# Strassen's seven products in the first product of the second FFN, on one Trainium2 core

## The chip, the cores and the metric

The kernel runs on one core of one Trainium2 chip. The metric is the device time of one execution in microseconds (us); the time before is the median of three runs. Engines are named as in the profile: PE is the matrix engine (TensorE), PEld its weight loads, DVE the vector engine (VectorE), ACT the scalar engine (ScalarE), SP the engine that issues the DMAs (SyncE).

## The reference

Three stages over 4608 tokens (8 batches of 576), a model width of 512 and an FFN width of 2048, all in fp32:

```
# linear attention, per batch and head, then RMS norm
kv  = einsum('bhsd,bhse->bhde', k, v);  out = einsum('bhsd,bhde->bhse', q, kv)
x   = out / sqrt(mean(out*out, -1) + 1e-6) * g_norm
# first FFN
h = x @ w_in;  g = P(h) / Q(|h|);  x = g @ w_out
# second FFN (the change is here)
h = x @ w_in                        # 4608x512 @ 512x2048
g = where(h >= 1, h, where(h <= -1, 0, (h + 1)**2 / 4))
return g @ w_out                    # 4608x2048 @ 2048x512
```

## The kernel before

**Tiles.** The tokens are cut into 9 blocks of T = 512 (`NB`), the FFN width into 16 slices of 128 (`NF`, index `f`), the model width into 4 slices of 128 (`KT`). An fp32 operand is kept as two fp32r tiles, a rounded high part and the rest (`xh`/`xl`, `wih`/`wil`, `woh`/`wol`, `gh`/`gl`), and a product of two operands takes three matmuls: high by high, high by low, low by high.

**The second FFN.** `ffn_step(1, j, f, s)` (L540) does for a block j and a slice f: 4 x 3 matmuls into one bank `h` (L548 to L550), the nonlinearity (a clamp on DVE, L577; a square on ACT; a maximum on DVE, L581), the split of g into `gh` (ACT) and `gl` (DVE, L199), and then 4 x 3 matmuls into the four banks `acc0` to `acc3` (L606 to L608), which sum over f. This second product lags by `LAG` = 3 steps: in(f) is followed by out(f-3). After f = 15 the banks are copied by ACT and stored. Everything in PSUM is 8 banks: two `h`, one `o`, one `m`, four `acc`; `o` and `m` serve the attention and are idle in the second FFN.

**Weights.** They come as 64-bit floats. `weight(ph, f, half, key)` (L254) loads one 512 KB slice into a `raw` tile, turns it into fp32 with integer and ACT instructions in a tile `t`, and splits it. For the second FFN (`ph` = 1) that takes one ACT conversion (L271), on DVE a shift (L274), the sign (L277) and the low bits (L282), the high part on ACT (L311) and the low part on DVE (L320). A slice's buffers become free as the last block of the first FFN passes it, so that the second FFN's weights are decoded during that block and during block 0 of the second FFN. All weights then stay in SBUF.

**Order.** No order of instructions is written by hand. Each operation is given to `Program` with its engine, a cost, a key (its due time in steps of 24 matmuls) and the buffers that it reads and writes. Buffers of one name form a ring of so many buffers, and within a ring they are handed on in the order of the buffers' keys: a later one waits for every operation on the one that it replaces. A list scheduler then plays the program through with its costs and, on each engine, always takes the ready operation of the smallest key:

```python
    LATENCY = 0.15
    ...
            while pending[e] and pending[e][0][0] <= s:
                i = heappop(pending[e])[1]
                heappush(ready[e], (self.ops[i][2], i))
            i = heappop(ready[e])[1]
```

The order that results is fixed for each engine, and each engine works through its own in order. All DMAs are issued by SP, in its order too. `NS1` = 144 is the key of the second FFN's first step. Inputs of the second FFN come back from DRAM (`x2d`) through three `io` buffers and are split by `x2_split` (L529); a split is one ACT instruction (high part) and one on DVE (low part).

Of the kernel before, what the change touches and what calls it, by code (L numbers as in the profile page):

```python
# [131 lines left out]
def kernel(  # L132
# [28 lines left out]
    T = 512  # L161
# [7 lines left out]
    const = ctx.enter_context(tc.tile_pool(name="const", bufs=1))  # L169
    sb = ctx.enter_context(tc.tile_pool(name="sb", bufs=1))  # L170
    psum = ctx.enter_context(tc.tile_pool(name="psum", bufs=1, space=bass.MemoryType.PSUM))

    RINGS = {
        "wih": NF, "wil": NF, "woh": NF, "wol": NF + 1, "raw": 4, "dec": 2, "io": 3, "xh": KT, "xl": KT,
        "gh": 2, "gl": 2, "ah": 1, "u": 2, "t": 2, "r": 2, "a1": 1, "a2": 1, "a3": 1, "a4": 1,
    }
    PS_RINGS = {"h": 2, "o": 1, "m": 1, "acc0": 1, "acc1": 1, "acc2": 1, "acc3": 1}
    count = [0]
# [75 lines left out]
    def weight(ph, f, half, key):  # L254
# [18 lines left out]
        def shift():  # L273
            nc.vector.tensor_scalar(out=t(), in0=t(), scalar1=3, scalar2=None, op0=ALU.logical_shift_left)  # L274

        def sign():
            nc.vector.scalar_tensor_tensor(  # L277
                out=t(), in0=word(1), scalar=-0x80000000, in1=t(), op0=ALU.bitwise_and, op1=ALU.bitwise_or
            )

        def low():
            nc.vector.scalar_tensor_tensor(  # L282
                out=t(), in0=word(0), scalar=29, in1=t(), op0=ALU.logical_shift_right, op1=ALU.bitwise_or
            )

        def low_bits():
# [11 lines left out]

        load(key, raw, (w1, w2)[ph][f, half], 1.4)
        op(ACT, 0.57, key, bias, [raw], [t])  # L300
        if ph == 0:

            lb = new("gl", key, I32)
            op(ACT, 0.57, key, low_bits, [raw], [lb])
            op(DVE, C_TT, key, shift_low, [lb], [t])
            op(DVE, C_TT, key, sign, [raw], [t])
        else:
            op(DVE, C_TS, key, shift, [], [t])
            op(DVE, C_TT, key, sign, [raw], [t])
            op(DVE, C_TT, key, low, [raw], [t])  # L310
        op(ACT, C_SB, key, lambda: nc.scalar.activation(out=hi(), in_=t().bitcast(F32), func=AF.Copy), [t], [hi])  # L311
        if keep:
            w32[f] = t
            wsb[ph, f, half] = (hi, None)
        else:
            weight_low(ph, f, half, key, t, hi)

    def weight_low(ph, f, half, key, t, hi):
        lo = new(("wil", "wol")[half], key, F32R)
# [2 lines left out]
        ), [t, hi], [lo])  # L322
        wsb[ph, f, half] = (hi, lo)


    xs = {}
    kvs = {}
# [85 lines left out]
    def x_split(e, xh, xl, key):  # L413
        activate(key, xh, e)
        subtract(key, xl, e, xh)
# [203 lines left out]

    NS1 = NB * NF

    order = [(0, 0), (1, 0), (2, 0)]
    for f in range(3, NF):
# [89 lines left out]
```

## Time and profile before

| | |
|---|---|
| median of three runs | 1680.24 us (1680.13 to 1683.94) |
| span of the profiled execution | 1677.8 us, first to last instruction |
| its own time | not printed; the median is 2.4 us above the span |
| busy: PE, DVE, ACT | 1655.2, 1187.1, 969.4 us |
| moved by DMA | 94.29 MB, 56 GB/s over the span |

Busy time is the time in which an engine has an instruction in hand; on PE and DVE consecutive instructions overlap, so that the distance between two starts is shorter than what one instruction lasts. A releaser is what ended an idle time: `<-DVE u L577` is an instruction of DVE on line 577 that wrote u.

### The profile page before, as it was taken

What the parts mean: (1) busy time and instruction counts of PE and PEld (TensorE: products, weight loads), DVE (VectorE), ACT (ScalarE), POOL (GpSimd) and SP (SyncE); (2) the same over time, 40 slices, a digit from 0 to 9 for tenths busy, and PEclk for the clock granted to TensorE, in tenths of its full rate; (3) what the DMA queues carried; (4) which work ended last, traced back from release to release, by engine and by line L of the source; (5) the groups of instructions that cost most, each with busy time, mean ns of one, the idle gap of its engine ahead of it and who ended that gap; (6) DMA issues with size and microseconds to landing.
All of it is one profiled execution on the core that took longest, in us unless ns stands there. A gap on an engine that the chain in (4) does not pass through costs nothing.

```text
span 1677.8 us, 20972 instructions
## 1 busy us (share of the span) xinstructions
PE 1655.2 (99%) x7888; PEld 1334.3 (80%) x7888; DVE 1187.1 (71%) x1864; ACT 969.4 (58%) x1633; POOL 0.2 (0%) x4
## 2 busy tenths in 40 slices
PE   6999999999999999999999999999999999999999
PEld 3666788888888888888888888888888888888887
DVE  5999999999999999999999953434343434343333
ACT  7987888887878788888886532323232323232222
POOL 0000000000000000000000000000000000000000
PEclk9999999999999999999999999999999999999999
DMA  8966101010101001010215410101010101000000
GB/s 276 308 215 190 39 19 39 19 38 19 38 20 38 11 11 49 26 45 13 76 51 169 144 51 0 51 1 51 0 51 1 50 1 51 1 25 7 1 26 25
DMA packets 51685, 94.29 MB, mean 56 GB/s; under 512 B 12992, under 2 KB 21056, under 8 KB 51584
## 3 DMA queue, kind: packets, MB, share of 16 engines
q1 hardware_dynamic: 51584, 92.96, 16.9%
q8 instruction: 62, 1.02, 0.2%
q14 instruction: 39, 0.32, 0.1%
HBM read 73.14 MB, written 19.79 MB: 55 GB/s over the span
## 4 chain that ended last, share of the span: by engine, by line
PE 95%; ACT 2%; DMA 2%; SPq 0%; DVE 0%; issue 0%; ACTq 0%
PE h L548 15%; PE h L549 15%; PE h L550 15%; PE acc L608 8%; PE acc L606 8%; PE acc L607 8%; PE acc L602 7%; PE acc L603 7%; PE acc L604 7%; PE acc L600 2%; DMA raw<-in_w_dram 1%; PE m L356 1%; PE o L501 1%; ACT a L194 0%; DMA wol<-in_kv_dram 0%; DMA ab_sb<-in_a_dram 0%
## 5 line engine op out<-in xcount | busy, mean ns | idle before, releaser
L548 PE MATMUL h<-xh,wih 128*128 128x512 f32 x1152 | 455.9, 396 | 3.7 <-DVE a L208 2.0
L549 PE MATMUL h<-xl,wih 128*128 128x512 f32 x1152 | 448.5, 389 | 0.0
L550 PE MATMUL h<-xh,wil 128*128 128x512 f32 x1152 | 448.4, 389 | 0.0
L194 ACT ACTIVATE u<-u 128x512 f32<-128x512 f32 x144 | 90.9, 631 | 352.2 <-DVE u L577 352.1
L548 PEld LDWEIGHTS h<-xh,wih 128*128 128x128 f32 x1152 | 216.1, 188 | 55.7 <-issue 4.2
L549 PEld LDWEIGHTS h<-xl,wih 128*128 128x128 f32 x1152 | 216.4, 188 | 47.2 <-issue 3.2
L550 PEld LDWEIGHTS h<-xh,wil 128*128 128x128 f32 x1152 | 216.2, 188 | 45.2
L577 DVE TENSOR_SCALAR u<-h 128x512 f32<-128x512 f32 x144 | 99.4, 691 | 180.3 <-PE h L550 180.3
L606 PE MATMUL acc<-woh,gh 128*128 128x512 f32 x576 | 224.1, 389 | 0.0
L607 PE MATMUL acc<-wol,gh 128*128 128x512 f32 x576 | 224.1, 389 | 0.0
L608 PE MATMUL acc<-woh,gl 128*128 128x512 f32 x576 | 224.1, 389 | 0.0
L602 PE MATMUL acc<-gh,woh 128*128 128x512 f32 x512 | 200.0, 391 | 0.0
L603 PE MATMUL acc<-gh,wol 128*128 128x512 f32 x512 | 199.3, 389 | 0.0
L604 PE MATMUL acc<-gl,woh 128*128 128x512 f32 x512 | 199.2, 389 | 0.0
L208 DVE SCALAR_TENSOR_TENSOR u<-u,r 128x512 f32<-128x512 f32 x272 | 186.9, 687 | 12.1 <-ACT r L194 8.3
L199 DVE TENSOR_TENSOR gl<-t,gh 128x512 fp32r<-128x512 f32 x144 | 99.6, 692 | 133.7 <-ACT gh L194 133.7
L194 ACT ACTIVATE gh<-t 128x512 fp32r<-128x512 f32 x144 | 90.9, 631 | 135.2 <-PE acc L607 134.3
L581 DVE TENSOR_TENSOR t<-u,h 128x512 f32<-128x512 f32 x144 | 99.0, 688 | 97.1 <-ACT u L194 97.1
L608 PEld LDWEIGHTS acc<-woh,gl 128*128 128x128 f32 x576 | 108.1, 188 | 22.6
L606 PEld LDWEIGHTS acc<-woh,gh 128*128 128x128 f32 x576 | 108.2, 188 | 22.4
L607 PEld LDWEIGHTS acc<-wol,gh 128*128 128x128 f32 x576 | 108.0, 188 | 22.4
L194 ACT ACTIVATE ah<-h 128x512 f32<-128x512 f32 x144 | 85.8, 596 | 66.2 <-PE h L550 65.1
(105 smaller groups left out, 2125.0 us busy)
## 6 DMA issues: line engine op xcount, KB each, us to landing
raw<-in_w_dram SPq DMA_DIRECT2D x64, 512.0 KB, 3.8
x2d<-io SPq DMA_DIRECT2D x36, 256.0 KB, 2.4
io<-x2d SPq DMA_DIRECT2D x36, 256.0 KB, 3.0
raw<-in_qT_dram SPq DMA_DIRECT2D x56, 128.0 KB, 3.0
raw<-in_kv_dram SPq DMA_DIRECT2D x12, 512.0 KB, 5.3
out_dram<-r SPq DMA_DIRECT2D x18, 256.0 KB, 2.0
out_dram<-a SPq DMA_DIRECT2D x18, 256.0 KB, 2.2
woh<-in_kv_dram SPq DMA_DIRECT2D x12, 256.0 KB, 5.2
```

What stands on the lines that cost most here:

```text
L194: op(ACT, cost, key, lambda: nc.scalar.activation(out=out(), in_=in_(), func=func, **{k: v() if callable(v) else v for k, v in kw.items()} ...
L199: op(DVE, C_TT, key, lambda: nc.vector.tensor_tensor(out=out(), in0=x(), in1=hi().bitcast(F32), op=ALU.subtract), [x, hi], [out])
L208: op(DVE, C_STT if callable(add) else C_TT, key, lambda: nc.vector.scalar_tensor_tensor(out=out(), in0=x(), scalar=add() if callable(add) ...
L548: nc.tensor.matmul(out=h(), lhsT=whi()[:, c], rhs=xh(), start=(p == 0), stop=False)
L549: nc.tensor.matmul(out=h(), lhsT=whi()[:, c], rhs=xl(), start=False, stop=False)
L550: nc.tensor.matmul(out=h(), lhsT=wlo()[:, c], rhs=xh(), start=False, stop=(p == KT - 1))
L602: nc.tensor.matmul(out=o(), lhsT=wohi()[:, c], rhs=gh(), start=first, stop=False)
L603: nc.tensor.matmul(out=o(), lhsT=wolo()[:, c], rhs=gh(), start=False, stop=False)
L604: nc.tensor.matmul(out=o(), lhsT=wohi()[:, c], rhs=gl(), start=False, stop=last)
L606: nc.tensor.matmul(out=o(), lhsT=gh()[:, c], rhs=wohi(), start=first, stop=False)
L607: nc.tensor.matmul(out=o(), lhsT=gh()[:, c], rhs=wolo(), start=False, stop=False)
L608: nc.tensor.matmul(out=o(), lhsT=gl()[:, c], rhs=wohi(), start=False, stop=last)
```

## The change

Blocks 1 to 8 of the second FFN are taken in four groups of two (block 0 stays as it was), and the slices in eight pairs. For a pair of slices, the two halves of the model width and the two blocks, the first product is a 2 x 2 by 2 x 2 product of blocks, done with seven products (Strassen's scheme in Winograd's form) of 2 x 3 matmuls each, into the banks `h`, `o` and `m`, which DVE reads and adds between the products (`ffn2_pair`). Four of the seven left operands are sums and differences of weight blocks. They are made once (`combine`), from the fp32 weights that are kept in DRAM (`td`), and are stored with the plain ones in DRAM (`wd`); each group streams all 56 tiles of 256 KB back through the `wih` ring (`stream`). The right operands are sums and differences of token blocks (`x_combinations`). Both blocks' g fall out of one pair, but there are only four `acc` banks. So one block's g goes on to the second product at once and the other's is kept in `raw` tiles and taken at the end of the half (`ffn2_group`): in the first eight slices the first block's is used and the second's kept, in the other eight the reverse, and the first block's two halves are added at the end. In `weight`, the second FFN's decode now takes the first FFN's path: the shift and one of the two bit operations on DVE give way to a second ACT conversion (L289) and one DVE instruction (L295). `kvbd` moves into the rings `kv0` and `kv1`, which are used again later.

```diff
+    wd = dram.tile([NPAIR, 7, P, T], F32, name="wd")
+    td = dram.tile([NF, P, T], F32, name="td")
...
-    kvbd = [fixed(f"kvbd{i}", [P, NP, P]) for i in range(2)]
+    kvbd = [new(f"kv{i}", -100, shape=(P, NP, P)) for i in range(2)]
...
-        t = new("wol" if keep else "dec", key, I32)
+        t = new("wol" if keep else f"a{1 + f % 4}" if ph and not half else "dec", key, I32)
...
+        lb = new(f"kv{half}", 0.5 * (key - NS1) - 20 + NS1, I32) if ph else new("gl", key, I32)
+        op(ACT, 0.57, key, low_bits, [raw], [lb])
+        op(DVE, C_TT, key, shift_low, [lb], [t])
+        op(DVE, C_TT, key, sign, [raw], [t])
...
+        if ph and not half:
+            store_plain(f, key + 0.3)
+            tds[f] = prog.buf(None)
+            op(SP, 0.7, key + 0.3, lambda: nc.sync.dma_start(out=td[f], in_=t().bitcast(F32)), [t], [tds[f]])
...
+    def combine(i, key):
+        a, b = (new(f"a{1 + (2 * i + n) % 4}", key) for n in range(2))
+        for t, f in ((a, 2 * i), (b, 2 * i + 1)):
+            load(key - 1, t, td[f], reads=[tds[f]])
+        s12, s34 = new("r", key), new("r", key + 0.01)
...
+        add(s12, 0, b, 0, b, 1, ALU.add, [b])
+        add(s12, 1, s12, 0, a, 0, ALU.subtract, [s12, a])
+        add(s34, 0, a, 0, b, 0, ALU.subtract, [a, b])
+        add(s34, 1, a, 1, s12, 1, ALU.subtract, [a, s12])
+        for n in range(4):
+            s, c = (s12, s34)[n // 2], q[n % 2]
+            stage = new("ah" if i < 2 else "dec", key + 2 + 0.01 * n, F32R)
... # high half on ACT (256 wide), low half on DVE (256 wide)
+            store(key, i, (S1 + n, S1 + n + 1), ...)
...
+    STREAM = (A11, S2, S1, A12, S3, A22, S4)
+    def stream(g, i, key):
+        for n, c in enumerate(STREAM):
+            t = new("wih", key + 7 + 0.01 * n, F32R)
+            op(SP, 0.7, key + 0.01 * n, lambda t=t, c=c: nc.sync.dma_start(out=t().bitcast(F32), in_=wd[i, c]),
+               [wds[i, c]], [t])
+            ws[g, i, c] = t
+    def x_combinations(g, key):
... # B11, T2, T1 in the wil ring, B21, T3, T4, B22 in xh and xl
+            split(B11, b11)
+            t1, t2 = (new("dec", k + 6 + 0.1 * n) for n in range(2))
+            sub(t1, b12, b11)
+            b22 = fetch(jb, 2 + i, 2)
+            sub(t2, b22, t1)
+            split(T2, t2)
+            split(T1, t1)
+            b21 = fetch(ja, 2 + i, 3)
+            split(B21, b21)
+            sub(b12, b22, b12)
+            split(T3, b12)
+            t4 = new(f"kv{i}", k + 4)
+            sub(t4, b21, t2)
...
+    def ffn2_pair(g, i, key):
+        banks = [new(r, key) for r in ("h", "o", "m")]
+        a, b, c = banks
+        v1, u2, u3 = new("t", key), new("kv0", key), new("kv1", key)
... # product(): 2 x 3 matmuls, cost 1.36, key + 0.01 * n;  add(): DVE, out = x + bank
+        product(0, a, A11, B11, True)
+        product(1, b, S2, T2, True)
+        product(2, c, S1, T1, True)
+        activate(key, v1, a, cost=C_PS)
+        add(u2, v1, b)
+        product(3, a, A12, B21, False)
+        product(4, b, S3, T3, False)
+        add(u3, v1, b)
+        add(u3, u3, c)
+        product(5, b, A22, T4, False)
+        product(6, c, S4, B22, False)
+        add(v1, v1, b)
+        add(u2, u2, c)
+        return (a, u2), (v1, u3)
...
+    def ffn2_group(g, s0):
+        ja, jb = 1 + 2 * g, 2 + 2 * g
+        STEP, LUMP = 2.92, 11.7
...
+        for half in range(2):
+            s = s0 + half * NF
+            for q in range(NPAIR // 2):
+                i = half * (NPAIR // 2) + q
+                k = s + STEP * q - 1.0
+                whole = new("raw", k + 3, shape=(P, 2 * T))
+                rows = ffn2_pair(g, i, k)
+                for n in range(2):
+                    f = 2 * i + n
+                    now, later = rows[n] if half == 0 else rows[n][::-1]
+                    ko = k + 3.3 + 1.4 * n
+                    keep = Half(whole, slice(n * T, (n + 1) * T))
+                    e = nonlinear(now, None, k + 0.5)
...
+                    ffn2_out(e, f, o4[0 if half == 0 else 1], ko, ...)
+                    kept.append((f, nonlinear(later, keep, k + 0.6)))
+            k = s + LUMP + 1.5
... # the four banks are copied by ACT, then the kept slices' second product
+            for n, (f, e) in enumerate(kept):
+                ffn2_out(e, f, o, k + 0.53 * n, n == 0, half == 1 and f == NF - 1)
...
-    for j in range(NB):
-        s0 = NS1 + j * NF
-        for p in range(KT):
-            x2_split(j, p, s0 - NF + 3 + 3 * p)
-        for f in range(NF):
-            ffn_step(1, j, f, s0 + f)
+    for p in range(KT):
+        x2_split(0, p, NS1 - NF + 3 + 3 * p)
+    for f in range(NF):
+        ffn_step(1, 0, f, NS1 + f)
+    for g in range((NB - 1) // 2):
+        s0 = NS1 + NF + 2 * NF * g
+        x_combinations(g, s0 - 6)
+        if g == 0:
+            for i in range(NPAIR):
+                combine(i, s0 + 2.0 * i - 5)
+        for i in range(NPAIR):
+            stream(g, i, s0 + (i // 4) * NF + 2.92 * (i % 4) - 7)
+        ffn2_group(g, s0)
```

`store_plain` stores A11, A12 and A22 (the plain blocks, high and low parts side by side) from the decoded tiles. `ffn2_out` is the split of g and the 4 x 3 matmuls of the second product as before, `nonlinear` the clamp, square and maximum as before.

## Rows read from the trace of the kernel before

**Rows 1.** The page's totals (busy us, share) and granted clock by slice.
```profile
PE 1655.2 (99%) x7888; PEld 1334.3 (80%) x7888; DVE 1187.1 (71%) x1864; ACT 969.4 (58%) x1633; POOL 0.2 (0%) x4
...
PEclk9999999999999999999999999999999999999999
```
**Rows 2.** The chain that ended last, by engine.
```profile
PE 95%; ACT 2%; DMA 2%; SPq 0%; DVE 0%; issue 0%; ACTq 0%
```
**Rows 3.** Busy time by stretch: PE, PEld, DVE, ACT, POOL; clock, DMA share, GB/s.
```profile
790.00:882.00 92.00, 92.00 (x408) 76.17 (x407) 91.47 (x152) 76.63 (x128) 0.00 (x0) 1.00 0.17 58
882.00:968.00 86.00, 86.00 (x382) 71.19 (x380) 83.86 (x150) 52.24 (x87) 0.00 (x0) 1.00 0.46 153
...
1011.00:1674.00 663.00, 663.00 (x2926) 548.64 (x2924) 265.30 (x388) 182.06 (x298) 0.00 (x0) 1.00 0.06 20
```
**Rows 4.** PE in order of time: start us, us, engine, line, operands.
```profile
963.92 0.39 PE L548 MATMUL h<-xh,wih 128*128 128x512 f32 x1
...
966.64 0.39 PE L606 MATMUL acc<-woh,gh 128*128 128x512 f32 x1
...
1301.20 0.39 PE L548 MATMUL h<-xh,wih 128*128 128x512 f32 x1
...
1303.92 0.39 PE L606 MATMUL acc<-woh,gh 128*128 128x512 f32 x1
...
1673.61 0.39 PE L608 MATMUL acc<-woh,gl 128*128 128x512 f32 x1
```
**Rows 5.** One step across engines, in order of time.
```profile
1303.69 0.39 PE L550 MATMUL h<-xh,wil 128*128 128x512 f32 x1
...
1304.12 0.69 DVE L577 TENSOR_SCALAR u<-h 128x512 f32<-128x512 f32 x1 [1.53 <-PE h L550]
...
1304.90 0.63 ACT L194 ACTIVATE u<-u 128x512 f32<-128x512 f32 x1 [3.04 <-DVE u L577]
...
1305.57 0.69 DVE L581 TENSOR_TENSOR t<-u,h 128x512 f32<-128x512 f32 x1 [0.76 <-ACT u L194]
```
**Rows 6.** DVE in order of time, around block 0's end.
```profile
940.03 0.42 DVE L274 TENSOR_SCALAR dec<-dec 128x512 int32<-128x512 int32 x1
940.37 0.69 DVE L199 TENSOR_TENSOR gl<-t,gh 128x512 fp32r<-128x512 f32 x1
940.97 0.68 DVE L320 TENSOR_TENSOR wil<-dec,wih 128x512 fp32r<-128x512 f32 x1
...
960.53 0.69 DVE L320 TENSOR_TENSOR wil<-dec,wih 128x512 fp32r<-128x512 f32 x1
...
973.36 0.68 DVE L199 TENSOR_TENSOR xl<-io,xh 128x512 fp32r<-128x512 f32 x1
973.96 0.68 DVE L577 TENSOR_SCALAR u<-h 128x512 f32<-128x512 f32 x1
975.40 0.69 DVE L581 TENSOR_TENSOR t<-u,h 128x512 f32<-128x512 f32 x1 [0.76 <-ACT u L194]
```
**Rows 7.** Groups of DVE instructions, 882 to 968: busy us, mean ns.
```profile
L274 DVE TENSOR_SCALAR dec<-dec 128x512 int32<-128x512 int32 x23 | 9.7, 421 | 0.0
```
**Rows 8.** DMA issues: KB each, median us to landing.
```profile
raw<-in_w_dram SPq DMA_DIRECT2D x64, 512.0 KB, 3.8
x2d<-io SPq DMA_DIRECT2D x36, 256.0 KB, 2.4
io<-x2d SPq DMA_DIRECT2D x36, 256.0 KB, 3.0
...
woh<-in_kv_dram SPq DMA_DIRECT2D x12, 256.0 KB, 5.2
```
**Rows 9.** Busy time by stretch, at the kernel's start.
```profile
10.00:20.00 10.00, 6.61 (x67) 4.41 (x67) 1.38 (x2) 2.67 (x6) 0.00 (x0) 1.00 0.94 313
...
60.00:80.00 20.00, 20.00 (x136) 12.58 (x134) 20.00 (x34) 19.90 (x38) 0.00 (x0) 1.00 0.99 332
```
**Rows 10.** Groups of ACT instructions, whole span: busy us, mean ns.
```profile
L289 ACT ACTIVATE gl<-raw 128x512 int32<-128x512 uint16 x32 | 21.4, 670 | 0.0
```
**Rows 11.** Busy time of 900 to 920, and SP's issues there.
```profile
900.00:920.00 20.00, 20.00 (x90) 16.57 (x89) 18.07 (x33) 11.87 (x21) 0.00 (x0) 1.00 0.69 230
...
902.04 0.32 SPq L616 DMA_DIRECT2D x2d<-io  x1
902.46 0.86 SPq L248 DMA_DIRECT2D io<-x2d  x2
```

More of the change, by code (lines that the diff above doesn't have):

```diff
@@ L618, in ffn_step, with fetch, sub, split @@
                     x2s[j, m] = stored
-    NS1 = NB * NF
+    ws = {}
+    xc = {}
+    B11, T2, T1, B21, T3, T4, B22 = range(7)
+    STREAM = (A11, S2, S1, A12, S3, A22, S4)
[7 more added lines that the diff above has]
+        ja, jb = 1 + 2 * g, 2 + 2 * g
+        for n, c in enumerate((B11, T2, T1)):
+            k = key + 0.1 * n
+            hl = [[new("wil", k + 6 + 0.01 * (2 * m + i), F32R) for i in range(2)] for m in range(2)]
+            xc[g, c] = hl
+        for n, c in enumerate((B21, T3, T4, B22)):
+            wholes = [new(r, key + 6.3 + 0.1 * n, F32R, (P, 2 * T)) for r in ("xh", "xl")]
+            xc[g, c] = [[Half(w, slice(i * T, (i + 1) * T)) for i in range(2)] for w in wholes]
+        late = []
+        for i in range(2):
+            k = key + 0.45 * i
+            def fetch(j, p, n, k=k):
+                t = new("io", k + 0.02 * n + (n == 4))
+                load(k + 0.02 * n, t, x2d[j, p], reads=[x2s[j, p]])
+                return t
+            def sub(out, x, y, k=k):
+                op(DVE, C_TT, k, lambda: nc.vector.tensor_tensor(
+                    out=out(), in0=x(), in1=y(), op=ALU.subtract), [x, y], [out])
+            def split(c, e, i=i, k=k):
+                x_split(e, xc[g, c][0][i], xc[g, c][1][i], k + 0.01 * c)
+            b11, b12 = fetch(ja, i, 0), fetch(jb, i, 1)
+            split(B11, b11)
[11 more added lines that the diff above has]
+            sub(t4, b21, t2)
+            late.append((split, fetch, t4))
+        for i, (split, fetch, t4) in enumerate(late):
+            split(T4, t4)
+            split(B22, fetch(jb, 2 + i, 4))
@@ new lines, in ffn2_pair, with product, mm, add @@
+    def ffn2_pair(g, i, key):
+        banks = [new(r, key) for r in ("h", "o", "m")]
+        a, b, c = banks
+        v1, u2, u3 = new("t", key), new("kv0", key), new("kv1", key)
+        def product(n, bank, wc, xn, start):
+            w = ws[g, i, wc]
+            xh, xl = xc[g, xn]
+            def mm():
+                for k in range(2):
+                    hi, lo = (w()[:, o + k * P:o + (k + 1) * P] for o in (0, HW))
+                    for m, (l, r) in enumerate(((hi, xh), (hi, xl), (lo, xh))):
+                        nc.tensor.matmul(
+                            out=bank(), lhsT=l, rhs=r[k](), start=(start and k == 0 and m == 0),
+                            stop=(k == 1 and m == 2), skip_group_check=True,
+                        )
+            op(PE, 1.36, key + 0.01 * n, mm, [w, *xh, *xl], [bank])
+        def add(out, x, bank):
+            op(DVE, C_TT, key, lambda: nc.vector.tensor_tensor(
+                out=out(), in0=x(), in1=bank(), op=ALU.add), [x, bank], [out])
+        product(0, a, A11, B11, True)
[12 more added lines that the diff above has]
+        return (a, u2), (v1, u3)
@@ new lines, in nonlinear, with ffn2_out, out_mm @@
+    def nonlinear(h, out, key):
+        cl = new("u", key)
+        op(DVE, C_TT, key, lambda: nc.vector.tensor_scalar(
+            out=cl(), in0=h(), scalar1=-1.0, scalar2=1.0, op0=ALU.max, op1=ALU.min
+        ), [h], [cl])
+        activate(key, cl, cl, AF.Square, scale=0.5, bias=0.5)
+        out = out or cl
+        op(DVE, C_TT, key, lambda: nc.vector.tensor_tensor(out=out(), in0=cl(), in1=h(), op=ALU.max), [cl, h], [out])
+        return out
+    def ffn2_out(e, f, o4, key, first, last):
+        gh, gl = new("gh", key - 0.8, F32R), new("gl", key - 0.8, F32R)
+        activate(key - 0.8, gh, e)
+        subtract(key - 0.8, gl, e, gh)
+        wohi, wolo = wsb[1, f, 1]
+        for m in range(4):
+            o = o4[m]
+            def out_mm(m=m, o=o):
+                c = slice(m * P, (m + 1) * P)
+                nc.tensor.matmul(out=o(), lhsT=gh()[:, c], rhs=wohi(), start=first, stop=False)
+                nc.tensor.matmul(out=o(), lhsT=gh()[:, c], rhs=wolo(), start=False, stop=False)
+                nc.tensor.matmul(out=o(), lhsT=gl()[:, c], rhs=wohi(), start=False, stop=last)
+            op(PE, 0.68, key, out_mm, [wohi, wolo, gh, gl], [o])
```

84 lines of the change are left out of this document (68 added, 16 removed).

## The prediction

> **What bounds the kernel now.** I read the page's totals first, then the chain of waits, then the span cut into stages, and only then single instructions. The totals put TensorE (PE) at 99% of the span with the clock granted in full in all 40 slices [rows 1], and the chain that ended last is 95% PE [rows 2]. The cut by stage says where something else comes near it [rows 3]: in the last block of the first FFN (790 to 882 us) and in block 0 of the second FFN (882 to 968) VectorE (DVE) is as full as PE (91.5 of 92 us and 83.9 of 86), and from 1011 us on, where the change does most of its work, DVE holds 265 of 663 us and ScalarE (ACT) 182. So in the second FFN after its first block, PE alone sets the time, and matmuls taken out there come out of the span as long as nothing makes PE wait.
>
> A matmul lasts 0.39 us in the trace, but that is not its price: twelve of them stand 2.72 us apart [rows 4], 0.2267 us each. Of a second-FFN block, 16 x 24 matmuls, that makes 87.04 us; eight blocks before the last one's final matmul (1673.6) lead back to block 0, whose last first product starts at 963.92 and ends at E = 966.6 [rows 4].
>
> **What is removed.** Over two f and two token blocks the first product now takes 7 products x 2 k x 3 = 42 matmuls in place of 4 x 12 = 48. The second product keeps its 12 for each f and block. Eight pairs of f and four pairs of blocks: 4 x 8 x 6 = 192 matmuls fewer, all of the same 128x512 form. 192 x 0.2267 = **43.5 us**. Block 0 and all of the first FFN keep their matmuls.
>
> **What is added in the steady part, and what covers it.**
> DVE: before, two blocks take 96 instructions of the nonlinearity and split plus 8 input splits, 104. After, a pair of blocks takes 8 x 5 adds, 64 of the nonlinearity, 32 splits, 22 of the input combinations and 4 final adds, 162. Back to back they start 0.60 us apart [rows 6]: 97.5 us against 720 x 0.2267 = 163.2 us of PE. DVE goes from some 40% to 60% and is no bound.
> ACT gains 8 copies and 6 splits per pair of blocks, each about 0.63 us [rows 5], beside 40% or less of load.
> DMA: 56 tiles of 256 KB per pair of blocks, 14.7 MB in 163 us, 90 GB/s. The core has moved 313 and 332 GB/s in stretches before [rows 9]. A load of that size lands in 3.0 us [rows 8], and the 16 buffers of wih hold 16/7 = 2.3 pairs of f, over 30 us of PE work. Hidden; without that lead each pair of f would wait one landing, 3 us.
>
> The new dependence is inside ffn2_pair. Bank b (o) is written, read and added to three times, c (m) twice, and each has one buffer. After the fifth product (the second into b), DVE must read b before the sixth product may add to it. From the rows: DVE starts 0.20 us after the last matmul's slot has ended (slot 1303.69 to 1303.92, start 1304.12), runs 0.69, and the next engine starts 0.09 later [rows 5]: 0.98 us. If DVE, which works in order, has just begun something else, 0.60 more. The other re-uses have two products (2.7 us) between write and re-use and need no cover. What covers the 1.0 to 1.6 us is the second product of the pair before: 8 groups of 3 matmuls, 0.68 us each, with later keys than the next pair's products, so that the planner takes them where a product isn't ready; two or three of the eight are needed. I cost this at 0. With the cover gone it is 1.0 to 1.6 us in each of 32 pairs.
>
> At half and group ends 8 f of kept g give 96 matmuls (21.8 us) that wait on no product. A split for the next of them (0.63 + 0.69 + 0.13 us [rows 5]) is shorter than the 2.72 us of the one that runs, and a bank's copy shorter than the three other banks' 2.04. The next group's combinations must wait for the last pair's products to free the buffers and run two loads deep through io's 3 buffers; I count about 9 us until the first product can go, under 16 us of outs. 0 too. At the end a DVE add (0.69) stands where an ACT copy did; nothing.
>
> **What is added at the changeover (about 930 to 1000 us), where DVE is full.** In the trace DVE's backlog lasts until 974.0, 7.4 us past E [rows 6], and the last wil is done 2.7 us before PE wants it (960.53 + 0.69 against 963.92). So each microsecond of DVE work there counts. Against the 23 weights decoded after 882 us [rows 7]:
> - the shift (TENSOR_SCALAR, 0.335 from start to start [rows 6]) goes: 23 x 0.335 = -7.7; block 1's four input splits go: -2.4;
> - the 22 instructions of the first combinations come: +13.2; two combines (of 8 half-width adds and splits each) fall ahead of weight 12 and 14 by their keys. No row shows a half-width two-input instruction; its bounds are 0.335 (that shift) and 0.60 (full width). I take 0.335, as half the columns: 16 x 0.335 = +5.4 (+9.6 at the upper end).
>
> Net +8.5 us (+12.8): the backlog would last until 982.5 (986.8). PE has, after E, the outs of f = 12 to 15 that lag by three steps: 4 x 2.72 = 10.9 us, to 977.5. The combinations' temporaries stand in the dec ring behind weights 13 and 14 of the second matrix, so those weights' decode isn't pushed back by them. PE's wait lies between 0 and 982.5 - 977.5 = 5.0 us (9.3 at the upper end); most combinations carry an earlier key than the last weight and get DVE first, so I take 3.
> ACT gets one more conversion for each weight (0.67 us [rows 10]): 23 x 0.67 = 15.4 and 6 more input splits, 3.8, on top of 52.2 of 86 us [rows 3]; 83%, still free.
> [...]
>
> **Sum.** The profiled execution's own time isn't printed; its span is 1677.8, and the median of the runs is 2.4 above it, which I let stand around both. 1677.8 - 43.5 + 3 = 1637.3 of span, **1639.7 us** of time.
>
> **Rivals.**
> *The changeover is bound by round trips through DRAM, not by DVE's count.* The combined weights of the first two pairs pass through one ah buffer, stage after stage: ACT 0.3 to 0.6 (half or all of a full-width one), DVE 0.34 to 0.6, a store. A 256 KB store lands in 2.4 us, and about 3.5 us a stage makes 14 us for a combine, just under the 15 us that a pair's 66 matmuls last. But where the queues were full at the start of the kernel such transfers took 5.2 us [rows 8, 9], and here 6.3 MB of plain stores, 4.2 of td stores, 2.1 of td loads, 4.2 of the combined weights' stores and 4.2 of first stream tiles, 21 MB in some 130 us, come on top of 153 GB/s over block 0 and 230 at its peak [rows 3, 11]. At 6.2 us a stage, 25 us a combine, the two that start about 938 (before weight 12, whose wil is at 940.97 [rows 6]) end at 988, and the next two, with two buffers, at 1013. Block 0's results leave two of their banks through r, behind combine 3 in that ring, so the first outs of the group would start near 1014; PE has outs and two pairs' products until 977.5 + 2 x 9.5 = 996.5. A loss of 18 us there; 8 to 25 as a range: 1680.2 - 43.5 + 18 = **1655**. For it: DMA busy 0.69 in 900 to 920 [rows 11]. Against it: the landing of raw, twice the size, has a median of 3.8 [rows 8], and a load issued 0.4 us after a store to the same DRAM tensor did not wait for it [rows 11].
> [...]
>
> *PE waits in every pair; slower than before.* The point from which this decides is 43.5 / 32 = 1.36 us of PE wait per pair of f. Were the out groups not there when the sixth product is due (held back by gh and gl, or by acc), and DVE two instructions behind, the wait is 0.98 + 2 x 0.60 = 2.2 us, 32 x 2.2 = 70: **1707**. For it: one buffer each for o and m, and DVE in order at 60%. Against it: eight groups for two or three needed.
>
> *It doesn't pay: the freed time is filled by waits of 1.2 to 1.5 us per pair.* The same place at about the price of the uncovered chain (1.0 to 1.6 us): **1680**. It needs the cover gone in nearly every pair.
>
> **Chances.** Forecast 0.77 (1636.7 to 1645, its wait from 0 to 8), round trips 0.16 (1645 to 1662), no gain 0.02, slower 0.05. The range 1635.5 to 1657 leaves out the two last and the upper end of round trips (0.04), 0.11 in all. A change of 0.3%, 5 us, is what a measurement can tell here: faster 0.93, same 0.02, slower 0.05.
>
> **What the profile after would show.** Matmuls: 192 fewer, PE still at 0.2267 spacing. PE's idle time near 965 to 1000 is the changeover's price (3 forecast, 18 by the round-trip rival, then with DMA or an r or ah buffer as releaser). From 1020 us on, PE idle ahead of the product lines (o or m, released by DVE) of under 0.1 us per pair if the cover holds, and 1 us or more if it doesn't. DVE near 60% busy there, DMA near 90 GB/s. The prediction is wrong if PE's waits sum to over 10 us in the pairs, if the matmul spacing grows, or if block 0 itself (882 to 966) stretches because weights come late.

## The result, and the profile of the changed kernel

The changed kernel takes 1651.82 us (median of four runs, 1650.20 to 1652.88) against 1680.18 us (1679.16 to 1683.94) for the kernel before: a ratio of 0.9822, interval 0.9808 to 0.9836. That is 28.4 us less. The sum had put 1639.7; the range held the result, but the narrow range of the likeliest case (1636.7 to 1645) did not. The result lies where the rival of the round trips was put.

The page of the changed kernel: the span, the totals, and the chain that ended last by engine.

```profile
span 1648.4 us, 21708 instructions
...
PE 1616.4 (98%) x7696; PEld 1298.5 (79%) x7696; DVE 1312.4 (80%) x2128; ACT 1023.7 (62%) x1753; POOL 0.2 (0%) x4
...
PE 86%; DVE 5%; DMA 5%; ACT 2%; issue 1%; SPq 0%; ACTq 0%; DVEq 0%
```

PE's matmuls fall from 7888 [rows 1] to 7696, which is exactly 192. But the chain is no longer PE nearly alone: 95% of it was [rows 2], now 86%, with DVE and DMA at 5% each. Something other than matmuls has come onto the path. All that PE waits for after 880 us (engine, operand and line, what it waited for: us in total, times, longest):

```profile
PE o L753 <- DVE kv L761: 3.7, 3, 1.8
PE h L601 <- ACT wih L304: 3.0, 1, 3.0
PE acc L801 <- DVE gl L205: 0.9, 2, 0.6
PE h L603 <- DVE wil L317: 0.4, 1, 0.4
PE h L601 <- DVE t L634: 0.4, 1, 0.4
PE acc L661 <- DVE gl L205: 0.3, 1, 0.3
```

These are nine waits and 8.7 us. PE in order of time shows where they are and what else the changeover costs (start, duration, engine, line, operands; in brackets the idle time ahead and its releaser):

```profile
965.30 0.39 PE L661 MATMUL acc<-woh,gl 128*128 128x512 f32 x1
968.67 0.50 PE L601 MATMUL h<-xh,wih 128*128 128x512 f32 x1 [2.97 <-ACT wih L304]
...
970.40 0.63 PE L601 MATMUL h<-xh,wih 128*128 128x512 f32 x1
970.83 0.63 PE L602 MATMUL h<-xl,wih 128*128 128x512 f32 x1
971.25 0.63 PE L603 MATMUL h<-xh,wil 128*128 128x512 f32 x1
...
990.17 0.50 PE L753 MATMUL o<-xh,wih 128*128 128x512 f32 x1 [0.85 <-DVE kv L761]
990.51 0.40 PE L753 MATMUL o<-xl,wih 128*128 128x512 f32 x1
...
1024.25 0.50 PE L753 MATMUL o<-xh,wih 128*128 128x512 f32 x1 [1.76 <-DVE kv L761]
...
1644.13 0.39 PE L801 MATMUL acc<-woh,gl 128*128 128x512 f32 x1
```

The last matmul starts at 1644.13 where it started at 1673.61 [rows 4], 29.5 us earlier; the first output product of block 0 starts 0.9 us later than before (902.28 against 901.36), so the stretch between the two is 30.4 us shorter. 43.5 - 30.4 leaves **13.1 us** lost inside the second FFN. Adding up what each gap between matmul starts has over 0.2267 us finds nearly all of it again: about 6 us from 959 to 973, 0.5 at 980, 2.45 at 990 to 993, 2.2 at 1024, and 1.4 in the whole rest to the end: 12.6. That is more than the 8.7 us of waits in the list, for three reasons. A wait in the list counts from the end of the matmul ahead, 0.39 us after its start, while its slot is over after 0.2267. The first matmul after a wait lasts 0.50 and the next starts 0.34 later (990.17, 990.51). And after the longest wait matmuls stand 0.43 us apart for a while (970.40, 970.83, 971.25). The windows show what that last one is (PE, PEld, DVE, ACT, POOL; granted clock, DMA share, GB/s):

```profile
900.00:920.00 20.00, 20.00 (x90) 16.56 (x89) 18.12 (x30) 15.77 (x29) 0.00 (x0) 1.00 0.94 336
940.00:960.00 20.00, 19.60 (x88) 15.91 (x86) 14.48 (x27) 10.85 (x21) 0.00 (x0) 1.00 0.92 302
970.00:972.00 2.00, 2.00 (x5) 1.61 (x6) 2.00 (x4) 1.40 (x3) 0.00 (x0) 0.50 0.88 247
980.00:1000.00 20.00, 18.08 (x77) 14.18 (x78) 19.96 (x37) 11.49 (x22) 0.00 (x0) 1.00 0.64 211
1059.00:1222.00 163.00, 162.38 (x717) 134.16 (x716) 101.42 (x165) 55.39 (x93) 0.00 (x0) 1.00 0.40 125
```

In 970 to 972 the granted clock is 0.50, against 1.00 in the other four windows, right behind the wait of 2.97 us. More telling is 940 to 960: DVE, which the prediction had full there, is busy 14.5 of 20 us, while the DMA share is 0.92, and 0.94 in 900 to 920 where it was 0.69 [rows 11]. DVE has become idle in the stretch where it was the bound. DVE in order of time says for whom it waits:

```profile
943.15 0.42 DVE L360 TENSOR_TENSOR r<-a,a 128x256 f32<-128x256 f32 x1
943.49 0.69 DVE L630 TENSOR_SCALAR u<-h 128x512 f32<-128x512 f32 x1
...
946.69 0.69 DVE L293 SCALAR_TENSOR_TENSOR dec<-dec,kv 128x512 int32<-128x512 int32 x1 [2.18 <-ACT kv L287]
...
1022.50 0.42 DVE L360 TENSOR_TENSOR r<-a 128x256 f32<-128x256 f32 x1 [2.59 <-DMA a<-td]
...
1023.51 0.68 DVE L761 TENSOR_TENSOR kv<-t,o 128x512 f32<-128x512 f32 x1
```

At 946.69 it is ACT (L287), and ACT in turn has waited for a weight's raw load, just ahead of that instruction and again at the last weight:

```profile
945.45 0.66 ACT L277 ACTIVATE dec<-raw 128x512 f32<-128x512 f32 x1 [3.08 <-DMA raw<-in_w_dram]
...
964.70 0.68 ACT L277 ACTIVATE a<-raw 128x512 f32<-128x512 f32 x1 [0.74 <-DMA raw<-in_w_dram]
...
967.98 0.63 ACT L304 ACTIVATE wih<-a 128x512 fp32r<-128x512 f32 x1 [0.42 <-DVE a L280]
```

From 885 to 972 us ACT's conversions (L277) wait 14.7 us in all for raw loads. The load at the root of the longest wait stands late in SP's order, behind stores and stream loads of the new traffic. Its issue, and two of the things that SP waits for in 885 to 972 (us in total, times, longest):

```profile
960.26 0.33 SPq L333 DMA_DIRECT2D wd<-ah  x1
960.65 0.92 SPq L254 DMA_DIRECT2D raw<-in_w_dram  x2
```

```profile
SPq L683 <- DMA wd<-ah: 9.9, 8, 2.5
SPq L333 <- DVE ah L373: 8.2, 7, 2.7
```

The first of the two is the round trip itself: a stream load (L683) waits at SP until the store of the combined tile has landed. The second is a store that waits for DVE to write the tile. Whatever stands behind them in SP's order waits too. So the chain reads: the store at 960.26, for which SP stood 1.3 us; raw issued at 960.65, landed at 964.70 (4.05 us), decoded by ACT and DVE, converted at 967.98, first matmul at 968.67. This load landed in little more than the 3.6 us of the kernel before: it came late because it was issued late. The second place, 984 to 993, is what the prediction described: DVE full (19.96 of 20 us), the banks' additions queued between the combinations. The third, 1024, is a combine whose tile landed late: DVE, in order, stands 2.59 us at 1022.50, and the bank's addition that PE wants (1023.51) is queued behind it. The DMA issues of 885 to 972 (KB each, median us to landing):

```profile
raw<-in_w_dram SPq DMA_DIRECT2D x19, 512.0 KB, 5.4
wih<-wd SPq DMA_DIRECT2D x15, 256.0 KB, 4.4
...
a<-td SPq DMA_DIRECT2D x8, 256.0 KB, 4.7
```

The same raw loads landed in 3.6 us in this stretch of the kernel before, so they take 1.8 us longer here (5.4 - 3.6); no run shows in what part of a transfer the 1.8 us arise.

### The profile page after: what moved, and what is told of

The parts are those of the page before. It is cut to its first block, busy times and chain, and to the rows that moved or that the text cites. A ratio compares the mean times of both kernels' runs of the same rounds, so it can differ in the third digit from the quotient of the medians.

```text
span 1648.4 us, 21708 instructions
## 1 busy us (share of the span) xinstructions
PE 1616.4 (98%) x7696; PEld 1298.5 (79%) x7696; DVE 1312.4 (80%) x2128; ACT 1023.7 (62%) x1753; POOL 0.2 (0%) x4
## 2 busy tenths in 40 slices
DMA packets 100973, 178.26 MB, mean 108 GB/s; under 512 B 18240, under 2 KB 32448, under 8 KB 100864
## 4 chain that ended last, share of the span: by engine, by line
PE 86%; DVE 5%; DMA 5%; ACT 2%; issue 1%; SPq 0%; ACTq 0%; DVEq 0%
PE h L601 8%; PE h L602 8%; PE h L603 8%; PE o L753 7%; PE acc L655 7%; PE acc L656 7%; PE acc L657 7%; PE acc L801 7%; PE acc L800 6%; PE acc L799 6%; PE m L753 5%; PE h L753 5%; PE acc L653 2%; DMA raw<-in_w_dram 2%; PE m L409 1%
## 5 line engine op out<-in xcount | busy, mean ns | idle before, releaser
L601 PE MATMUL h<-xh,wih 128*128 128x512 f32 x640 | 257.4, 402 | 7.3 <-ACT wih L304 3.0
L603 PE MATMUL h<-xh,wil 128*128 128x512 f32 x640 | 250.0, 391 | 0.4 <-DVE wil L317 0.4
L602 PE MATMUL h<-xl,wih 128*128 128x512 f32 x640 | 249.8, 390 | 0.0
L200 ACT ACTIVATE gh<-u 128x512 fp32r<-128x512 f32 x192 | 121.0, 632 | 66.0 <-PE acc L800 27.2
L205 DVE TENSOR_TENSOR gl<-u,gh 128x512 fp32r<-128x512 f32 x192 | 131.4, 686 | 30.3 <-ACT gh L200 22.2
L601 PEld LDWEIGHTS h<-xh,wih 128*128 128x128 f32 x640 | 120.6, 188 | 40.3 <-ACT wih L304 3.6
L602 PEld LDWEIGHTS h<-xl,wih 128*128 128x128 f32 x640 | 120.5, 188 | 27.2 <-issue 3.2
L603 PEld LDWEIGHTS h<-xh,wil 128*128 128x128 f32 x640 | 120.5, 188 | 26.2 <-DVE wil L317 0.8
L200 ACT ACTIVATE u<-ah,absb 128x512 f32<-128x512 f32 x144 | 117.4, 815 | 0.0
L655 PEld LDWEIGHTS acc<-gh,woh 128*128 128x128 f32 x512 | 96.1, 188 | 21.3 <-ACT ah L200 1.0
L657 PEld LDWEIGHTS acc<-gl,woh 128*128 128x128 f32 x512 | 96.1, 188 | 20.0
```

The source lines that it names most:

```text
L200: op(ACT, cost, key, lambda: nc.scalar.activation(out=out(), in_=in_(), func=func, **{k: v() if callable(v) else v for k, v in kw.items()} ...
L601: nc.tensor.matmul(out=h(), lhsT=whi()[:, c], rhs=xh(), start=(p == 0), stop=False)
L602: nc.tensor.matmul(out=h(), lhsT=whi()[:, c], rhs=xl(), start=False, stop=False)
L603: nc.tensor.matmul(out=h(), lhsT=wlo()[:, c], rhs=xh(), start=False, stop=(p == KT - 1))
L655: nc.tensor.matmul(out=o(), lhsT=wohi()[:, c], rhs=gh(), start=first, stop=False)
L657: nc.tensor.matmul(out=o(), lhsT=wohi()[:, c], rhs=gl(), start=False, stop=last)
```

## The experiments

Three theories stood against each other for the 13.1 us. **Bytes:** the combine's traffic fills the DMA queues, and weights come late. **Round trip:** the store and re-load through DRAM, one waiting for the other, is the chain. **Work:** DVE simply has too much to do, as the forecast's wait was derived. A fourth question was whether the steady pairs really lose nothing.

**1. The combine without its traffic.** The tiles of td are zeroed on GpSimd instead of loaded, nothing is stored to td, the combined tiles aren't stored, and the stream loads A11 in their place; DVE's and ACT's work stays.

```diff
-            load(key - 1, t, td[f], reads=[tds[f]])
+            op(POOL, 1.0, key - 1, lambda t=t: nc.gpsimd.memset(t(), 0.0), [], [t])
...
-            store(key, i, (S1 + n, S1 + n + 1), ...
```

> Leaves out the combined weights' way through DRAM: combine works on zeros that GpSimd writes, its results are not stored, td is neither stored nor loaded, and the stream brings the plain block A11 in their place, so that the numbers that come out are not the reference's. All of combine's DVE and ACT instructions stay, and the 56 stream tiles too. If the loss at the changeover comes from transfers that land late, PE's waits before 1060 us, some 12 us now, fall under 3 us and the time is about 1641 us. If it comes from the count of DVE work there, the waits stay at 8 us or more and the time at 1648 us or more.

Measured: 1643.46 us in one run (before beside it: 1680.53). What PE waits for after 880 us (the lines are four lower than in the changed kernel):

```profile
PE h L749 <- DVE t L630: 2.5, 1, 2.5
PE acc L797 <- DVE gl L205: 0.8, 1, 0.8
PE o L749 <- DVE kv L757: 0.2, 1, 0.2
```

Without the traffic 8.4 us come back. What remains is 3.5 us of waits, all for DVE and 2.5 of them in one place near 970, close to the 3 us forecast from DVE's work; behind that wait matmuls stand 0.45 us apart until 973, some 1.5 us more. The traffic is most of the loss; bytes, round trip and the order that they bring with them are all still possible.

**2. The plain stores later.** If SP's order is the trouble, moving the stores of the plain weights behind should give time back.

```diff
-            store_plain(f, key + 0.3)
+            store_plain(f, key + 0.3 + (8 if f >= 8 else 2))
```

> Same work and bytes; the plain blocks' stores get a later due time (by 2 steps for the first eight slices, 8 for the others), so that raw loads go ahead of them in SP's order. If late raw loads hold the last weights and PE behind them, raw loads land in under 4.6 us, PE's waits at the changeover fall to 0 to 5 us, and the time is 1640 to 1645 us. If DVE's count of work sets the changeover, nothing moves: 1650 to 1653 us.

Measured: 1649.15 us (1648.07 to 1651.42), ratio 0.9814 (0.9799 to 0.9828): some 2.7 us, where 7 to 12 were expected, and the runs of the two kernels overlap, so that even this gain is not clear of the noise. The raw loads of 885 to 972 land in 5.4 us as before, not in under 4.6. The wait for weight 15 was gone, but five waits of `PE h L601 <- DVE t L634` (3.0 us) and one of 2.1 at L753 had come in their place, with DMA share at 0.89 in 930 to 972. A miss: moving one kind of transfer moved the waits, it did not remove them.

**3. Three plain blocks, three groups.** Blocks 1 and 2 take the old step, so the combines come two blocks (2 x 87 us) later: DVE's work on them (L360, L373) runs from 1082 to 1218 us, where no weight is decoded any more. 144 matmuls fewer than before instead of 192.

```diff
-    for g in range((NB - 1) // 2):
...
+    for j in range(3):
+        for f in range(NF):
+            ffn_step(1, j, f, NS1 + j * NF + f)
+    for g in range(1, (NB - 1) // 2):
...
-        if g == 0:
+        if g == 1:
```

> Blocks 0 to 2 by the old step, three pairs of blocks by seven products: 144 matmuls fewer than before in place of 192, 32.6 us, and two blocks more of time for the combined weights. If the whole loss sits at the changeover, this kernel has next to none: 1680.2 - 32.6 + 1 = 1648.6 us (1647 to 1651), as fast as the changed kernel or faster with 48 matmuls more. If every pair loses a part, three quarters of the 28.4 us are won: 1659 us.

Measured: 1649.52 us (1649.38 to 1649.83), ratio 0.9814 (0.9797 to 0.9830). All PE waits after 880 us come to 1.0 us. 144 x 0.2267 = 32.6, and 31.0 came out: three groups of pairs run at nearly their full saving. Nearly the whole loss is the changeover's, and the steady part's rival (a wait in every pair) is out.

**4. The cover taken away, first try.** All output products of the pair before are put ahead of the fifth product.

```diff
+        prog.ops[-1][4].update(ahead)
+        ahead.clear()
...
+            ahead.append(len(prog.ops) - 1)
```

> All second-product matmuls of the pair before are put ahead of the fifth product of each pair of slices, so that none is left to fill PE's wait for bank o behind it; nothing else is changed. By the prediction's working the wait that comes to light is 1.0 to 1.6 us in each of 32 pairs, 31 to 51 us, and the time 1683 to 1703 us, no better than before the change. If the re-use of the banks costs next to nothing anyway, the time rises by under 6 us, to at most 1658 us.

Measured: 1689.25 us in one run, 37 us above the changed kernel. The size is as expected, but the place isn't: only 5.1 us of PE's waits are at o, more are at acc (8.0 behind gl, 5.2 behind gh). The next pair's first product had slipped in between the fifth and the sixth as another cover. It shows that the order matters by tens of us, not yet what one uncovered re-use costs; run 10 does that.

**5. The same bytes without the round trip.** The combine loads tiles of x2d, which were written long before, in place of td, and the stream loads A11 in place of the combined tiles; every transfer is still made, but none waits for a store of the combine. Two things stay: the stream's plain tiles still wait for their own stores, and a tile of ah is still re-used only when its store has landed.

```diff
-            load(key - 1, t, td[f], reads=[tds[f]])
+            load(key - 1, t, x2d[0, f % KT])
...
-               [wds[i, c]], [t])
+               [wds[i, c if c in (A11, A12, A22) else A11]], [t])
```

> Every transfer of the changed kernel stays, with its size, but none waits for one that went through DRAM before it: combine loads x2d in place of td, and the stream brings the stored A11 in place of the combined weights, so that the numbers that come out are not the reference's. If the bytes are what is too much for the DMA engines between 900 and 1040 us, PE loses there what it loses now, 9 to 14 us, and the time is 1648 to 1653 us. If the store and load back to back is what is late, it loses 5 us or less: 1645 us or less.

Measured: 1654.54 us in one run, span 1652.8: no gain at all. Two windows (columns as above):

```profile
930.00:972.00 42.00, 38.57 (x164) 30.36 (x163) 35.03 (x63) 28.64 (x53) 0.00 (x0) 0.99 0.93 325
972.00:1016.00 44.00, 40.26 (x153) 30.81 (x152) 38.23 (x69) 23.98 (x44) 0.00 (x0) 0.89 0.65 211
```

With the reload's dependence gone and the bytes kept, PE is idle 7.2 of 86 us and DVE still waits (35.0 of 42 us busy). Raw's median landing in 885 to 972 is 6.0 us. SP no longer waits for wd<-ah to land, but its waits for DVE to write ah rise from 8.2 to 13.8 us, and behind the raw load at 950.21 the next goes out at 960.25 (950.08 and 960.65 in the changed kernel). PE's waits after 880 us sum to 7.8 us against 8.7, and matmuls 0.43 us apart, in 972 to 975 and 996 to 1002, cost some 4 us against 1.5. So the reload's dependence by itself isn't the cause. The bytes and the order in which they are sent are both still there.

**6. A plan that knows of it.** If late landings in an order made for early ones are the cause, an order made for later landings should keep the bytes and lose the waits. The planner counted 2.1 us from the end of a DMA's issue to its data, and 0.7 or 1.4 us of issue.

```diff
-            free[e] = s + cost
+            free[e] = s + cost * (1.15 if e == SP else 1.0)
...
-                late = 2.1 if e == SP else ...
+                late = 2.3 if e == SP else ...
...
-        load(key, raw, (w1, w2)[ph][f, half], 1.4)
+        load(key - (4 if ph else 0), raw, (w1, w2)[ph][f, half], 1.4)
...
-            store_plain(f, key + 0.3)
+            store_plain(f, key + 0.3 + (6 if f >= 8 else 0))
...
-                combine(i, s0 + 2.0 * i - 5)
+                combine(i, s0 + 2.4 * i + -5)
...
-            stream(g, i, s0 + (i // 4) * NF + 2.92 * (i % 4) - 7)
+            stream(g, i, s0 + (i // 4) * NF + 2.92 * (i % 4) - 4)
```

> The same instructions and bytes in another order: the scheduler is told that a transfer takes 15% longer and lands 0.2 us later, raw loads get a due time 4 steps earlier, the plain stores of the last eight slices one 6 steps later, the stream tiles one 3 steps later, and the combines are spread at 2.4 steps instead of 2.0. If DMA engines are over-full only because of what is sent when, PE's wait at the changeover falls under 4 us and the time is 1638 to 1643 us. If the sum of bytes in the stretch decides, it stays above 1647 us.

Measured: 1644.16 us (1642.78 to 1644.84), ratio 0.9781 (0.9766 to 0.9796), just above the 1638 to 1643 expected. One wait is left, and PE in order of time shows what follows it:

```profile
969.92 0.79 PE L601 MATMUL h<-xh,wih 128*128 128x512 f32 x1 [2.58 <-ACT wih L304]
...
972.08 0.63 PE L602 MATMUL h<-xl,wih 128*128 128x512 f32 x1
972.51 0.63 PE L603 MATMUL h<-xh,wil 128*128 128x512 f32 x1
```

and in DVE's and ACT's what makes it:

```profile
964.64 0.43 DVE L360 TENSOR_TENSOR r<-r,a 128x256 f32<-128x256 f32 x1 [1.25 <-DMA a<-td]
...
965.43 0.68 ACT L277 ACTIVATE a<-raw 128x512 f32<-128x512 f32 x1 [1.93 <-DVE r L360]
...
969.24 0.63 ACT L304 ACTIVATE wih<-a 128x512 fp32r<-128x512 f32 x1 [3.13 <-DVE a L280]
```

A combine's td tile landed 5.2 us after its issue at 959.39, DVE waited for it, and weight 15's decode, whose tile is in the same a ring, waited for DVE. The wait is 2.6 us, and behind it matmuls stand 0.43 us apart until 975.5.

**7 and 8. The two halves of run 6.** Its keys with the planner's old numbers, and its numbers with the old keys.

> The due times of the other order (raw loads, plain stores, stream, combines), with the scheduler's costs as they were. If the costs by which the scheduler reckons transfers are what is wrong, this gains little: 1646 to 1651 us. If due times alone are at fault, it is at 1638 to 1643 us.

> Only the scheduler's costs of transfers are changed (15% longer, 0.2 us later), all due times as they were. If the costs alone were at fault, the time is 1638 to 1643 us. If due times put the wrong transfers first whatever the costs, it gains little: 1646 to 1651 us.

Measured: keys alone 1650.46 us (1648.99 to 1652.44), ratio 0.9820 (0.9806 to 0.9835); numbers alone 1652.78 us (1651.74 to 1654.25), ratio 0.9831 (0.9815 to 0.9848). The first is 1.4 us below the changed kernel, the second 1.0 above, and the runs of both overlap with the changed kernel's: neither half is told from no gain. The two together gain 7.7. The wait isn't in one place that one shift mends.

**9. Run 6 with later landings.** The plan of run 6 still counted 2.3 us to landing, on top of 0.7 or 1.4 us of issue, so 3.0 or 3.7 in all, where 4.6 to 5.2 were measured from issue to landing.

```diff
-            free[e] = s + cost * (1.15 if e == SP else 1.0)
+            free[e] = s + cost * (1.1 if e == SP else 1.0)
...
-                late = 2.3 if e == SP else ...
+                late = 3.6 if e == SP else ...
```

> The other order of due times again, with the scheduler told of a landing 3.6 us after a transfer's own time (2.1 in the changed kernel, 2.3 in the run before) and of 10% more time for each (15% before): the raw, td and stream loads there land in 4.6 to 5.2 us. If DVE's and ACT's waits on late td loads, in order, are what held the last weight in the run before, PE's waits after 880 us fall under 1.5 us in all, the clock stays at its upper level, and the time is 1637.5 to 1640.5 us. If the bytes in the stretch still don't fit, PE waits for a weight again, 2 us or more, and the time is 1643 us or more.

Measured: **1640.01 us** (1639.12 to 1642.05, five runs), ratio **0.9756** (0.9743 to 0.9769); it is faster than both kernels. Its one PE wait after 880 us, and its windows:

```profile
PE m L753 <- DVE wil L205: 0.6, 1, 0.6
```

```profile
930.00:972.00 42.00, 41.38 (x183) 33.96 (x182) 41.45 (x75) 29.13 (x54) 0.00 (x0) 1.00 0.94 315
972.00:1016.00 44.00, 43.99 (x195) 36.03 (x194) 35.57 (x70) 23.04 (x44) 0.00 (x0) 1.00 0.84 282
```

The same 178.26 MB are moved as in the changed kernel, the DMA share in 930 to 972 is as high as ever (0.94), and raw's median landing is 5.3 us. Yet DVE is now busy 41.45 of 42 us and PE 41.38. So neither the bytes nor the slow landings cost the time by themselves; they cost it in an order that doesn't allow for them. From run 6 to this one only the planner's two numbers differ, and that is 4.2 us.

What the order changes can be read at SP, in 885 to 972 as above:

```profile
SPq L254 <- DVE a L280: 15.7, 7, 3.8
...
SPq L683 <- DMA wd<-ah: 1.0, 1, 1.0
```

L280 is the last instruction that reads a raw tile: raw loads now stand first in SP's order and wait only for their buffer. The last two go out at 946.4, where the changed kernel sends four after 960. The round trip and the stores of ah hold SP for 3.0 us (1.0 and 2.0) instead of 18.1. Early raw loads are not enough, though: in run 7 the last one goes out at 952.2, and PE still waits 7.4 us, all of it for DVE. The order also moves DVE's work on the first two combines, which ends at 984 instead of 965; no run here tells these two effects apart.

**10. The price of an uncovered re-use.** Run 9's kernel, with nothing of PE between the fifth and the sixth product: the pair before has its outputs ahead of the fifth, and its own outputs and the next pair's first product come after the seventh (the edit of run 4, with those made to depend on the seventh product).

> The kernel of the run before it in this call, with nothing left to stand between the fifth and the sixth product of a pair: the second product's matmuls of the pair before come ahead of the fifth product, the pair's own ones and the next pair's first product behind the seventh. By the prediction's working PE waits 1.0 us for DVE's read of bank o in each of 32 pairs (1.6 where DVE has just begun something else), and as the next pair's first product may not run ahead either, some 6 us more at each change of groups: 45 to 70 us more than that kernel. If the re-use of bank o is hidden without cover, the wait per pair is under 0.3 us.

Measured: 1705.02 us in one run, 65 us above run 9. PE's waits, and PE at one such place:

```profile
PE o L754 <- DVE kv L762: 24.2, 31, 0.8
PE acc L804 <- ACT gh L200: 15.1, 4, 4.0
PE acc L804 <- ACT r L200: 5.9, 2, 3.7
```

```profile
1306.77 0.39 PE L754 MATMUL o<-xh,wih 128*128 128x512 f32 x1
1307.93 0.50 PE L754 MATMUL o<-xh,wih 128*128 128x512 f32 x1 [0.78 <-DVE kv L762]
```

31 of the 32 pairs wait, and the gap is 1307.93 - 1306.77 = 1.16 us, 0.93 over a spacing. 31 x 0.93 is 29 us. Of the rest, 15.1 us are at the group changes, where outputs have no product to hide behind (four waits of up to 4.0 us), and 5.9 us at 1000 to 1007, where the group's first outputs wait for block 0's results to be copied into r; matmuls stand 0.43 us apart behind those two waits. What is left of the 65 us isn't followed here.

## Why the prediction was right, and which term was off

**The saving: right.** 192 matmuls went, at an unchanged spacing (twelve in 2.72 us, 1396.84 to 1399.56 in the changed kernel, 0.2267 each). Run 9, where next to nothing waits, is 40.8 us below its kernel before (1680.82 - 1640.01); of the 43.5 it lacks 2.7, 0.6 of it in its one wait. In its profiled run 13 matmuls fewer than in the kernel before have been started by 890 us (4417 against 4430), 2.9 us, so that most of what it lacks lies ahead of the changeover. The sum's 1639.7 lies near this kernel, not near the changed one, and in part by luck: its 3 us stood for a wait that is 0.6 here. It also added 2.4 us outside the span, where the runs that print both show 1.8 (1650.20 against a span of 1648.4).

**The steady pairs at 0: right.** From 1059 us to the end PE loses 1.4 us in all, and run 3 finds nothing more either. The uncovered price was put at 0.98 and measured 0.93 (run 10). DVE's share in 1059 to 1222 is 62% (60 forecast). DMA moves 125 GB/s there; the 90 forecast were the stream's alone, 20 were there already [rows 3], and eight more input loads of 256 KB in this window make 13.

**A half-width DVE instruction: right.** It starts 0.34 us before the next (943.15, 943.49 in the changed kernel); 0.335 was taken.

**The wait at the changeover: wrong, 3 us forecast against some 12.** The failing step is the one that worked it out from DVE's work alone: DVE's backlog to 982.5 against PE's cover to 977.5, at most 9.3. That step took DVE as full, because it was full before (83.9 of 86 us [rows 3]). In the changed kernel it isn't: 77.05 of 87 us in 885 to 972, and 14.5 of 20 in 940 to 960. It waits for ACT, which waits for raw loads that SP issues behind the new traffic and that take 5.4 us to land instead of 3.6; later it waits for td's tiles, with the banks' additions queued behind. Run 1 prices that traffic, with the waits that it brings to SP, at 8.4 us; the sum had no term for it. What run 1 leaves at the changeover is 4.7 us over the matmuls' spacing, 1.5 of them in matmuls 0.45 us apart. Run 9 gives DVE its work in time; then it is full, as the step assumed, and PE waits 0.6. So DVE's work by itself was worth 0.6 to 4.7 us, and the step's 3 stood for that alone. One of the prediction's own signs of being wrong came true: block 0 stretched because a weight came late (its last first product starts at 968.67 instead of 963.92 [rows 4]).

**The rival of the round trips: right on the load and on the pace of its chain, wrong on what the chain holds up.** It named the transfers under load (21 MB more in 130 us), put a landing near 5 us, and its loss of 8 to 25 holds the 13.1 measured. It put a stage through the one ah buffer at 6.2 us; DVE's eight instructions on ah (L373) start at 925.16 to 964.28 in the changed kernel, 5.6 us apart. But the chain starts some 13 us before its 938, and block 0's results behind combine 3 in r aren't what bound: the group's first output matmul starts at 1001.90 (1014 by the rival), and no PE wait of that kernel is for r. In run 9 the chain is even slower (932.94 to 984.05, 7.3 us a stage), and PE waits 0.6. Only run 10, with the cover gone, shows that wait for r, 5.9 us. What the stages did hold up is SP, and behind it the raw loads: 18.1 us in 885 to 972. Taking one half of that away moved the other and gained nothing (run 5); taking both away with the traffic (run 1), or putting raw loads first in an order that allows for late landings (run 9), gave most of the loss back. Of the two arguments against this rival, the first, that raw's median landing was 3.8 [rows 8], was read from a kernel with a DMA share of 0.46 in that block [rows 3], and the change took the share to 0.86 there (885 to 972). The second, a load that didn't wait for a store [rows 11], was a load of another block's tile; a stream load does wait for the store of its own.

**Not told ahead: the clock.** A wait of 2.97 us in the changed kernel and one of 2.58 us in run 6, each in the middle of a full stretch, were followed by a granted clock of 0.50 and by matmuls 0.43 us apart instead of 0.2267. That cost 1.5 us in the changed kernel (970 to 973) and some 3 us in run 6.

Open: which of run 6's keys are needed (they were tried as a whole), whether run 9's numbers would do with the old keys, and how much of the 13.1 us is the landings, how much SP's order and how much DVE's; they act on each other, as runs 6 to 9 show. A combine that doesn't pass through DRAM at all was not tried.

## What to carry to other kernels

Where PE alone set the time here, a matmul taken out was worth nearly its spacing (40.8 us for 192 in run 9, where 192 x 0.2267 is 43.5), and the re-used banks cost next to nothing (1.4 us from 1059 us to the end of the changed kernel) as long as independent groups stood between a bank's write and its re-use; check that they can, since taking them away cost 65 us, 29 of them at the bank itself. Before putting new traffic into a stretch where another engine is full, recount the DMA share and re-read the landing times as they will be under that share (from 3.6 us at 0.46 to 5.4 at 0.86 here): the engine that was full, 84.86 of 87 us in 885 to 972, came to wait instead (77.05), and its old busy time no longer told the price. Where one engine issues all transfers in order, look at what it waits for as well: SP stood 18.1 us in 885 to 972 for stores of ah that weren't ready and for loads that wait for them, with raw loads behind. And an order planned ahead depends on the landing times in its plan: the same bytes and the same work took 1651.8 us with 2.1 us of landing in the plan, and 1640.0 us with 3.6 and keys that fit it, while new keys alone (1650.5 us) or a small change of the numbers alone (1652.8) gained nothing clear.

## What the runs showed of the hardware

**A wait of 2 to 3.5 us cost twice.** After the 2.97 us wait of the changed kernel the granted clock is 0.50 in 970 to 972; after the 2.58 us wait of run 6 it is 0.50 from 970 to 976. Matmuls then stand 0.43 us apart (970.40, 970.83, 971.25) instead of 0.2267. The same spacing follows single waits of 1.96 us (run 5), 2.12 (run 2), 2.50 (run 1), 2.55 (run 7) and 3.53 (runs 4 and 8). After the 1.76 us wait at 1024 the clock is granted in full (1.00 in 1024 to 1026), and so it is after 1.68 us in run 7 (965.50; 1.00 in 930 to 972). The length of the last wait alone doesn't tell, though: in run 5 matmuls stand 0.43 us apart (996.04, 996.47) after a wait of 1.40 us, with waits of 0.67 and 0.77 us not long before.

**The first matmul after a wait at full clock lasted 0.50 us and the next started 0.33 to 0.34 later** (968.67, 990.17, 1024.25), so that a short wait too cost 0.1 us more than its gap.

**Sixteen DMA engines at a share of 0.92 to 0.95** moved 300 to 336 GB/s here, with 5147 of 13472 packets under 2 KB in 885 to 972 of the changed kernel. In that stretch a 512 KB load landed in 5.4 us (median) at a share of 0.86, in 5.3 in run 9 at 0.87, in 6.0 in run 5 at 0.86 and in 4.6 in run 6 at 0.82, against 3.6 at 0.46 in the kernel before.
